# Coefficient tile allocated ahead of the weight pool: every weight tile starts 32 bytes later

## Chip, cores and metric

The kernel runs on one core of one Trainium2 chip. The metric is device time in microseconds of one execution. Before the change three runs took 1612.5, 1613.8 and 1614.32 us; their median, 1613.8 us, is the time to compare with.

## What is computed

Three stages run one after the other on 6016 tokens (2 sequences of 3008), all in float32:

```
scores = (1/S) * z @ z.T            # z: 3008 x 64 per sequence
x  = u * (max(scores, 0)**2 @ v)    # u, v: 3008 x 256 per sequence
h  = x @ w_in1                      # 256 -> 2048
x  = where(h > 0, h, exp(min(h, 0)) - 1) @ w_out1     # 2048 -> 256
h  = x @ w_in2
g  = (a0 + a1*h + a2*h^2 + a3*h^3) / (1 + |b0|*|h| + |b1|*h^2 + 1e-6)
out = g @ w_out2
```

The weights come as float64. The six coefficients a0 to a3, b0, b1 are scalars.

## The kernel before

Each float32 product is made of three matmuls on pairs of tiles: every operand is held as a rounded part (hi) and a remainder (lo), and hi*hi, hi*lo and lo*hi are added in PSUM. So TensorE (PE) issues 9240 matmuls, each with a weight load of its own (PEld).

The stationary operand of a matmul is `lhsT`, the moving one is `rhs`. In this kernel they come from these places:

- Scores (`scores`, L292): both operands are slices of the split z tiles, which lie in pool `sp` (names rl, x, t, r). The contraction is 64 long, so two matmuls stand side by side, one on the lower and one on the upper 64 rows. A pair is one step of the array.
- Attention times v (`values`, L329): stationary is the split v, which lies in pool `wp` (name w); moving is the squared score (hl and x, in `sp`). Again pairs of 64 rows.
- The two feed-forward layers (`hidden`, L399 to L402, and `project` with `mm3`, L263 to L265): stationary is a split weight in `wp` (w); moving is the activation in `sp` (rl, hl, x). The contraction is 128 long, and there are no pairs.
- In the last token tile alone the second layer's result also goes into tiles of `wp` (`second` with form "last"), so that there both operands of L263 to L265 are named w (`psum<-w`).

The moving operand is 512 columns wide in most of the work. In the attention each sequence is cut into five blocks of 512 and one of 448. In the feed-forward layers the tokens are cut into nine tiles of 512 columns and then one each of 448, 384, 320 and 256. A tile passes 16 groups (fewer of double width in the narrow ones), and the second layer of a tile runs beside the first layer of the next.

Pools are laid out in SBUF in the order in which they are entered, and the tiles of a pool behind each other. `wp` holds 32 tiles of 4096 bytes in each partition, `cp` one tile of 24 bytes that takes up 32 (`coef`), `sp` all the rest, in tiles of 2048 or 4096 bytes. The order of the instructions is written out by the code itself (`tc.manual_schedule()`); no planner depends on addresses.

Of the kernel before, what the change touches and what calls it, by code (L numbers as in the profile page):

```python
# [21 lines left out]
def attention_then_two_ffns(  # L22
# [56 lines left out]
    NG = [NF // g for g in PER]  # L79
    NSL = -(-S // W)  # L80

    wp = ctx.enter_context(tc.tile_pool(name="wp", bufs=32))
    cp = ctx.enter_context(tc.tile_pool(name="cp", bufs=1))
    sp = ctx.enter_context(tc.tile_pool(name="sp", bufs=2))
    dp = ctx.enter_context(tc.tile_pool(name="dp", bufs=1, space=bass.MemoryType.DRAM))
    ps = ctx.enter_context(tc.tile_pool(name="ps", bufs=1, space=bass.MemoryType.PSUM))
# [739 lines left out]
```

## Time and profile before

| | before |
|---|---|
| median of three runs | 1613.8 us |
| span of the profiled execution | 1611.0 us |
| PE busy | 1569.5 us, 97% of the span |
| DVE (VectorE) busy | 1392.3 us, 86% |
| ACT (ScalarE) busy | 1326.0 us, 82% |
| POOL (GpSimd) busy | 723.9 us, 45% |

The page gives the profiled execution's span, from the first to the last instruction; the 2.8 us up to the median of the runs lie around it. The attention takes the time up to about 521 us, the feed-forward layers the rest; the tiles narrower than 512 columns begin at about 1269 us with the first layer of the 448-wide one. Matmuls overlap: the duration of one is longer than the distance to the next. What a matmul costs a busy PE is the distance from start to start, which the view of instructions in order of time gives. There each row is a run of equal instructions with its start, the time to the last end, and the count.

### The profile page before, as it was taken

The numbers are of one execution on the slowest core, as the hardware profiler recorded it, in microseconds if no ns is written. First come the engines' busy times: TensorE is split into PE (matmuls) and PEld (weight loads), VectorE is DVE, ScalarE is ACT, GpSimd is POOL, SyncE is SP. The second block draws the span as 40 slices with busy tenths as digits, with TensorE's granted clock in tenths as the row PEclk, the third lists the DMA queues.
The fourth block names the chain that finished last, engine by engine and source line by source line (L and its number), as shares of the span: only waits on it lengthen the run. The fifth ranks groups of instructions, "written<-read, shape, count | busy, mean of one in ns | idle before, by whom it ended". The sixth has DMA issues, their size and how long they took to land.

```text
span 1611.0 us, 25201 instructions
## 1 busy us (share of the span) xinstructions
PE 1569.5 (97%) x9240; PEld 1321.5 (82%) x9240; DVE 1392.3 (86%) x1915; ACT 1326.0 (82%) x2123; POOL 723.9 (45%) x590
## 2 busy tenths in 40 slices
PE   8999999999999999999999999999999999999986
PEld 6888897898778778787878787887878888999976
DVE  7788889888886478989898988889898999999998
ACT  6777776877776788988888888988888888999886
POOL 3344542443433444445444444444454444444445
PEclk9999999999999999999999999999999999999999
DMA  4243343221222400000000000000000000000000
GB/s 125 66 125 119 112 144 109 66 68 50 75 61 89 157 26 1 27 1 1 27 1 27 1 27 1 27 0 1 25 1 23 1 22 1 20 1 12 11 1 15
DMA packets 38716, 67.16 MB, mean 42 GB/s; under 512 B 4928, under 2 KB 15680, under 8 KB 38592
## 3 DMA queue, kind: packets, MB, share of 16 engines
q1 hardware_dynamic: 38592, 65.55, 13.1%
q8 instruction: 72, 1.18, 0.3%
q14 instruction: 52, 0.43, 0.1%
HBM read 45.88 MB, written 19.66 MB: 41 GB/s over the span
## 4 chain that ended last, share of the span: by engine, by line
PE 66%; DVE 11%; issue 3%; ACT 3%; POOL 1%; POOLq 0%; ACTq 0%; DVEq 0%
PE psum L329 11%; PE psum L264 9%; PE psum L399 9%; PE psum L402 9%; PE psum L265 9%; PE psum L400 9%; PE psum L263 9%; PE psum L292 3%; DVE x L526 2%; DVE t L528 1%; DVE q L503 1%; DVE q L527 1%; DVE e L432 1%; DVE t L509 1%; ACT t L480 1%
## 5 line engine op out<-in xcount | busy, mean ns | idle before, releaser
L533 POOL TENSOR_TENSOR x<-t,r 128x512 fp32r<-128x512 f32 (+3 forms) x190 | 233.9, 1231 | 509.4 <-DVE t L528 443.3
L329 PE MATMUL psum<-hl,w 64*128 64x512 f32 (+1 forms) x2256 | 395.2, 391 | 3.7 <-ACT xo L349 2.6
L329 PEld LDWEIGHTS psum<-hl,w 64*128 64x128 f32 x2256 | 279.7, 185 | 44.4 <-ACT xo L349 6.4
L329 PE MATMUL psum<-x,w 64*128 64x512 f32 (+1 forms) x1128 | 293.1, 388 | 1.0 <-DVE x L305 1.0
L441 POOL TENSOR_TENSOR hl<-e,hl 128x512 fp32r<-128x512 f32 (+3 forms) x200 | 246.8, 1234 | 35.4 <-ACT hl L440 29.6
L295 ACT ACTIVATE w<-psum 128x1024 f32<-128x1024 f32 (+1 forms) x144 | 145.5, 1011 | 111.3 <-PE psum L292 109.8
L298 DVE SCALAR_TENSOR_TENSOR psum<-psum,w 128x1024 f32<-128x1024 f32 (+1 forms) x144 | 173.8, 1207 | 57.9 <-ACT w L295 57.2
L480 ACT ACTIVATE t<-psum,coef 128x512 f32<-128x512 f32 (+3 forms) x200 | 150.6, 753 | 78.8 <-PE psum L402 77.4
L503 DVE SCALAR_TENSOR_TENSOR q<-q,coef,psum 128x512 f32<-128x512 f32 (+3 forms) x190 | 135.3, 712 | 72.1 <-ACT q L496 71.5
L305 DVE TENSOR_TENSOR x<-psum,hl 128x1024 fp32r<-128x1024 f32 (+1 forms) x144 | 172.9, 1201 | 12.0 <-ACT q L200 0.5
L329 PEld LDWEIGHTS psum<-x,w 64*128 64x128 f32 x1128 | 168.0, 185 | 17.3 <-DVE x L305 1.5
L264 PE MATMUL psum<-hl,w 128*128 128x512 f32 (+4 forms) x416 | 157.2, 378 | 4.8 <-POOL hl L441 4.5
L399 PE MATMUL psum<-x,w 128*128 128x512 f32 (+4 forms) x416 | 155.6, 376 | 2.0 <-ACT x L451 1.4
L264 PE MATMUL psum<-x,w 128*128 128x512 f32 (+3 forms) x384 | 147.8, 385 | 8.5 <-POOL x L533 8.5
L263 PE MATMUL psum<-hl,w 128*128 128x512 f32 (+4 forms) x416 | 155.6, 374 | 0.2 <-ACT hl L440 0.2
L399 PE MATMUL psum<-rl,w 128*128 128x512 f32 (+4 forms) x416 | 155.5, 376 | 0.0
L265 PE MATMUL psum<-hl,w 128*128 128x512 f32 (+4 forms) x416 | 155.3, 373 | 0.0
L400 PE MATMUL psum<-x,w 128*128 128x512 f32 (+4 forms) x416 | 154.7, 374 | 0.0
L400 PE MATMUL psum<-rl,w 128*128 128x512 f32 (+4 forms) x416 | 154.4, 373 | 0.0
L296 ACT ACTIVATE hl<-w 128x1024 fp32r<-128x1024 f32 (+1 forms) x144 | 150.6, 1046 | 4.6
L432 DVE SCALAR_TENSOR_TENSOR e<-e,psum 128x512 f32<-128x512 f32 (+3 forms) x200 | 129.8, 649 | 27.8 <-ACT e L427 21.8
L526 DVE SCALAR_TENSOR_TENSOR x<-t,coef,r 128x512 fp32r<-128x512 f32 (+3 forms) x190 | 150.2, 791 | 0.0
(143 smaller groups left out, 3683.2 us busy)
## 6 DMA issues: line engine op xcount, KB each, us to landing
raw<-w_in_dram SPq DMA_DIRECT2D x16, 512.0 KB, 3.9
raw<-w_out_dram SPq DMA_DIRECT2D x16, 512.0 KB, 3.8
wd<-q SPq DMA_DIRECT2D x28, 256.0 KB, 2.3
raw<-wd SPq DMA_DIRECT2D x14, 512.0 KB, 3.4
raw<-v_dram SPq DMA_DIRECT2D x22, 256.0 KB, 2.9
raw<-uT_dram SPq DMA_DIRECT2D x10, 512.0 KB, 3.8
xd<-xo SPq DMA_DIRECT2D x20, 256.0 KB, 2.2
outT_dram<-xo SPq DMA_DIRECT2D x18, 256.0 KB, 2.2
```

The source lines that it names most:

```text
L263: nc.tensor.matmul(out, lhsT=lh, rhs=rh, start=start, stop=False)
L264: nc.tensor.matmul(out, lhsT=lh, rhs=rl, start=False, stop=False)
L265: nc.tensor.matmul(out, lhsT=ll, rhs=rh, start=False, stop=stop)
L298: nc.vector.scalar_tensor_tensor(out=s, in0=s, scalar=SCALE, in1=e, op0=ALU.mult, op1=ALU.mult)
L305: nc.vector.tensor_tensor(out=lo[:, :, :w], in0=psum[:, i:i + 2, :w], in1=f(hi[:, :, :w]), op=ALU.subtract)
L329: nc.tensor.matmul(acc[ti][d, h][:, :w], lhsT=lhs[rows, j % 2, d * P:(d + 1) * P], rhs=rhs[rows, :w], start=j == 0 and k == 0, stop=k == 2 ...
L399: nc.tensor.matmul(h[:, cols], lhsT=wh[:, d, c], rhs=x[d][0], start=d == 0, stop=False)
L400: nc.tensor.matmul(h[:, cols], lhsT=wl[:, d, c], rhs=x[d][0], start=False, stop=False)
L441: nc.gpsimd.tensor_tensor(out=lo, in0=e, in1=f(hi), op=ALU.subtract)
L480: act(new("p", "t", 3), h, AF.Identity, bias=a2, scale=a3)
L526: stt(out=st["hi"], in0=st["top"], scalar=a0, in1=st["r"], op0=ALU.add, op1=ALU.mult)
L533: eng.tensor_tensor(out=st["lo"], in0=st["p"], in1=st["r"], op=ALU.mult)
```

## The change

Two lines change places: pool `cp` is entered before pool `wp` instead of behind it.

```diff
+    cp = ctx.enter_context(tc.tile_pool(name="cp", bufs=1))
     wp = ctx.enter_context(tc.tile_pool(name="wp", bufs=32))
-    cp = ctx.enter_context(tc.tile_pool(name="cp", bufs=1))
     sp = ctx.enter_context(tc.tile_pool(name="sp", bufs=2))
```

The instructions of all five engines are the same, row for row and in the same order. Only addresses in SBUF differ. In the built programs they are (bytes in a partition):

```
            before                          after
coef        147584          (128 mod 512)   16512           (128 mod 512)
wp          16512 + 4096*i  (128 mod 512)   16544 + 4096*i  (160 mod 512)
sp          147616 ...      (160 mod 512)   147616 ...      (160 mod 512)
```

Slices of these tiles that a matmul reads start at multiples of 512 bytes in the tile. So before, a stationary operand in `wp` lies at 128 modulo 512 and a moving one in `sp` at 160; after, both lie at 160. The scores had both at 160 already, and still have. The last tile's `psum<-w` matmuls had both at 128 and have both at 160.

## Rows read from the trace of the kernel before

**Rows 1.** The page: busy time and share of each engine; chain by engine.

```profile
PE 1569.5 (97%) x9240; PEld 1321.5 (82%) x9240; DVE 1392.3 (86%) x1915; ACT 1326.0 (82%) x2123; POOL 723.9 (45%) x590
PE 66%; DVE 11%; issue 3%; ACT 3%; POOL 1%; POOLq 0%; ACTq 0%; DVEq 0%
```

**Rows 2.** Windows: start:end, length, busy us (count) by engine, clock, DMA, GB/s.

```profile
100.00:522.00 422.00, 414.54 (x3527) 359.30 (x3524) 359.30 (x373) 314.94 (x381) 177.75 (x141) 1.00 0.30 92
740.00:830.00 90.00, 89.95 (x386) 72.06 (x385) 80.07 (x118) 78.28 (x132) 42.65 (x33) 1.00 0.04 12
1280.00:1370.00 90.00, 89.85 (x412) 76.83 (x411) 83.24 (x126) 80.75 (x144) 42.17 (x35) 1.00 0.03 11
1370.00:1450.00 80.00, 79.01 (x416) 74.01 (x415) 75.83 (x126) 73.40 (x143) 37.56 (x35) 1.00 0.03 11
1520.00:1577.00 57.00, 47.98 (x335) 44.62 (x333) 54.68 (x101) 47.95 (x101) 22.17 (x23) 1.00 0.03 8
1578.50:1581.50 3.00, 3.00 (x15) 2.83 (x14) 2.90 (x5) 2.32 (x6) 2.93 (x3) 0.50 0.00 0
1582.00:1590.00 8.00, 7.93 (x67) 7.73 (x67) 7.26 (x11) 6.61 (x12) 5.19 (x4) 1.00 0.11 40
```

**Rows 3.** PE in order of time, attention, 512 columns: start, us, what, count.

```profile
15.46 0.86 PE L292 MATMUL psum<-rl 64*128 64x512 f32 x6
16.14 0.64 PE L329 MATMUL psum<-hl,w 64*128 64x512 f32 x4
16.61 0.40 PE L329 MATMUL psum<-x,w 64*128 64x512 f32 x2
...
18.94 0.86 PE L292 MATMUL psum<-rl,x 64*128 64x512 f32 x6
19.62 0.64 PE L329 MATMUL psum<-hl,w 64*128 64x512 f32 x4
```

**Rows 4.** PE in order of time, feed-forward layers, 512 columns.

```profile
900.01 0.40 PE L263 MATMUL psum<-x,w 128*128 128x512 f32 x1
...
902.35 0.63 PE L402 MATMUL psum<-x,w 128*128 128x512 f32 x2
902.81 0.40 PE L263 MATMUL psum<-hl,w 128*128 128x512 f32 x1
```

**Rows 5.** PE in order of time, attention, 448 columns.

```profile
222.98 0.81 PE L292 MATMUL psum<-r,rl 64*128 64x448 f32 x6
223.59 1.14 PE L329 MATMUL psum<-hl,w 64*128 64x448 f32 x4
...
485.55 0.78 PE L329 MATMUL psum<-hl,w 64*128 64x448 f32 x4
...
488.03 0.98 PE L292 MATMUL psum<-r,x 64*128 64x448 f32 x6
```

**Rows 6.** PE in order of time, last tile, 256 columns.

```profile
1579.26 0.42 PE L400 MATMUL psum<-x,w 128*128 128x256 f32 x1
...
1581.18 0.57 PE L402 MATMUL psum<-x,w 128*128 128x256 f32 x2
...
1584.44 0.28 PE L399 MATMUL psum<-x,w 128*128 128x256 f32 x1
...
1585.86 0.28 PE L263 MATMUL psum<-w 128*128 128x256 f32 x1
...
1592.76 0.28 PE L265 MATMUL psum<-w 128*128 128x256 f32 x1
...
1593.96 0.28 PE L263 MATMUL psum<-w 128*128 128x256 f32 x1
```

**Rows 7.** Groups by line and shape: count, busy us, mean ns, idle before.

```profile
L329 PE MATMUL psum<-hl,w 64*128 64x512 f32 x1880 | 337.3, 395 | 2.8 <-ACT xo L349 1.7 <-ACT hl L296 0.9
L329 PE MATMUL psum<-x,w 64*128 64x512 f32 x940 | 253.6, 392 | 1.0 <-DVE x L305 1.0
L329 PE MATMUL psum<-hl,w 64*128 64x448 f32 x376 | 57.9, 370 | 0.9 <-ACT xo L349 0.8
L329 PE MATMUL psum<-x,w 64*128 64x448 f32 x188 | 39.6, 365 | 0.0
L399 PE MATMUL psum<-rl,w 128*128 128x512 f32 x288 | 114.9, 399 | 0.0
L399 PE MATMUL psum<-rl,w 128*128 128x448 f32 x32 | 11.8, 369 | 0.0
```

## The prediction

> **What bounds the kernel now.** I read the page's busy line first, then windows stage by stage, then PE in order of time. TensorE is busy 97% of the span, and the chain that ended last runs through PE for 66% of it [rows 1]. In the middle of the feed-forward layers nothing else counts: in the window 740 to 830 us PE is busy 89.95 of 90 us at granted clock 1.00, with 386 matmuls, which is 90/386 = 0.2332 us for each [rows 2]. DVE is next with 80.07 of 90 us. In the attention PE is busy 414.54 of 422 us [rows 2]. Only in the last narrow tiles (47.98 of 57 us) does PE stand idle while DVE is nearly full (54.68 of 57) [rows 2]. So what matters is the distance from one matmul's start to the next, and the number of matmuls.
>
> The reader should look for the distance in the order of time, since the 0.40 us that a row gives for one matmul overlaps the next. Twelve matmuls of the feed-forward layers, from 900.01 to 902.81 us, take 2.80 us: 233.3 ns each [rows 4]. At the clock's upper level, 2.4 GHz, 512 columns are 213.3 ns, so 20 ns come on top. They are not a fixed part of a matmul: at the lower level (granted clock 0.50 in the window 1578.5 to 1581.5) nine 256-column matmuls between 1579.26 and 1581.18 us take 1.92 us, 213.3 ns each, which is 256 columns at 1.2 GHz and nothing more [rows 2, 6].
>
> **The change part by part.** No instruction, wait or DMA is added, removed or moved. coef keeps its offset modulo 512, `sp` keeps its addresses; all that can change is the speed of instructions that touch `wp`. The trace of before holds the case after already: the scores read both operands at 160 modulo 512, while the products with v read stationary ones at 128 and moving ones at 160. These two stand next to each other, same width, same 64-row pairs:
>
> - L292, both at 160: 15.46 to 16.14 us for 3 pairs, 226.7 ns a pair; again 18.94 to 19.62 us, 226.7 ns [rows 3].
> - L329, 128 against 160: 16.14 to 18.94 us for 24 matmuls or 12 pairs, 233.3 ns a pair [rows 3].
>
> The difference is 6.67 ns, 16 columns at 2.4 GHz. The 128-row matmuls of the feed-forward layers have the same 233.3 ns as the pairs with unequal offsets [rows 3, 4], so I take rows as without influence, and give them the same 6.67 ns. At 448 columns: both at 160, 222.98 to 223.59 us, 3 pairs, 203.3 ns; unequal, 485.55 to 488.03 us, 12 pairs, 206.7 ns [rows 5]: 3.3 ns. At 256 columns the sign turns: unequal, 1584.44 to 1585.86 us, 12 matmuls, 118.3 ns; both at 128, 1592.76 to 1593.96 us, 10 matmuls, 120.0 ns [rows 6]: 1.7 ns dearer. One reading fits most of it: with equal offsets a matmul costs its columns plus about 32, whatever the width (512: 544 columns are 226.7 ns; 256: 288 are 120.0 ns); with unequal ones the addition grows with the width, from 28 (118.3 ns) to 48 (233.3 ns).
>
> The sum, against the profiled execution's span of 1611.0 us:
>
> 1. Attention. L329 has 1880 + 940 = 2820 matmuls of 512 columns, 1410 pairs, and 376 + 188 = 564 of 448, 282 pairs [rows 7]. 1410 x 6.67 ns = 9.4 us, 282 x 3.3 ns = 0.9 us. PE is idle for 1.8% here and waits now and then on ACT and DVE, which do not get faster, so I let nine tenths through: 9.3 us. Bounds: 0 (others take it back) and 10.3.
> 2. Feed-forward, 512 columns. Twelve groups like L399's, each 288 [rows 7]: 3456 x 6.67 ns = 23.0 us. The cover to ask about is DVE: of a 90 us window it fills 80.07; in the 87.4 us which that window becomes (386 x 6.67 ns = 2.6 us less) it fills 91.6%. In the window 1280 to 1370 it fills 83.24 of 90, 92.5%, and PE still loses only 0.15 us [rows 2]. So all of it passes. Bounds: 23.0 more and 23.0 less, the latter if 128-row matmuls follow the 256-column row (third rival).
> 3. 448 columns. 12 x 32 = 384 matmuls [rows 7] x 3.3 ns = 1.3 us. Here DVE already fills 75.83 of 80 us and PE idles 1.0 [rows 2]: half, 0.6 us. Bounds 0 and 1.3.
> 4. 384, 320 and 256 columns, and the end. No row shows equal offsets at 384 and 320. The 256-column row gives +1.7 ns, the 448-column row -3.3 ns; for 384 matmuls of each of two widths that is +1.3 to -2.6 us, and for the 256-column ones (of 384, the 96 with both operands in w are equal already) 288 x 1.7 ns = +0.5 us. DVE sets the pace there, so I take 0.
> 5. Other engines. ACT, DVE and POOL read and write `wp` in the attention (the ReLU tile, the splits of v and the weights). They wait less than PE there: DVE 359.30 and ACT 314.94 of 422 us [rows 2]. Their instructions' durations could move either way by some ns; PE hides them. 0, bounds +-1 us.
>
> 9.3 + 23.0 + 0.6 = 32.9 us. Span 1611.0 - 32.9 = 1578.1 us; with the 2.8 us between span and median, 1580.9, say **1581 us**.
>
> **The rivals.**
>
> *No change: the offsets are not the cause.* Scores and products with v differ in more than the offset: the stationary operand of L292 lies high in SBUF with the moving one, that of L329 lies low, at 16512 to 147584. If the region decides, moving by 32 bytes does nothing and the time is 1613.8 us. Against it: 1.92 us for nine matmuls at the lower clock shows a loss that comes from two streams at speed, and region as such gives no reason why 256-column matmuls with both operands low should be the slower ones. The Trainium skill speaks for this rival: its page "SBUF — State Buffer", section "Who interferes with whom", gives TensorE two SBUF read ports, one for the moving operand and one for the weight load, that are independent, and says that PE never waits on anyone; by that rule an offset between the two could not matter. Its page "TensorE: Matmul & The Clock Gate", section "Back-to-back issue gap", gives columns/2.4 + 2.5 ns, 215.8 ns for 512. The trace does not agree: 226.7 and 233.3 ns at the same width and clock, with different operands.
>
> *Only the pairs gain.* All rows at 512 columns with equal offsets are 64-row pairs. If full-height matmuls gain nothing, term 1 alone stays: 1613.8 - 9.3 = 1604.5 us. Against it, 233.3 ns in both forms at unequal offsets.
>
> *Slower: equal offsets hurt full-height matmuls.* The only full-height rows with equal offsets are the 256-column ones, 120.0 against 118.3 ns. If their addition (32 on 256, one in eight) is a rate, 512 columns cost 576 columns, 240.0 ns: 3456 x 6.67 = 23.0 us lost in term 2, 9.3 gained in term 1, 1613.8 + 13.7 = 1627.5 us. It decides from 236.0 ns a matmul on, where 3456 x 2.7 ns eats the 9.3 us. Against it: 226.7 ns for L292 contradicts such a rate, unless pairs are apart.
>
> *The gain is taken back by DVE.* If PE, once faster, waits for DVE at its 91.6%, about half of term 2 goes: 9.3 + 11.5 + 0.3 = 21.1 us, 1592.7 us. Against it the window 1280 to 1370.
>
> **How the numbers follow.** Forecast 0.75, for itself 1574 (every term whole, with 2.6 us at 384 and 320 and 1 us from the others: 10.3 + 23.0 + 1.3 + 2.6 + 1 = 38.2, so 1575.6, and a little for the spread of the runs) to 1588 (terms 1 and 2 four fifths: 25.9). DVE rival 0.05, pairs only 0.07, no change 0.06, slower 0.07. The range from 1573 to 1600 us leaves out the last three, 0.20. Faster by over 0.2% (3.2 us, about what a measurement tells from no change): 0.75 + 0.05 + 0.07 = 0.87; within it 0.06; slower 0.07.
>
> **What would show it.** In order of time, L329 pairs at 226.7 ns like L292's and twelve feed-forward matmuls in 2.72 instead of 2.80 us; a 90 us window there with about 397 matmuls instead of 386 and DVE near 82.5 us; 256-column matmuls near 120 ns. The forecast is wrong if the 512-column feed-forward matmuls stay at 233 ns (first two rivals) or exceed it (third), or if they are at 226.7 ns but PE shows new waits on DVE or ACT (fourth).

## The result and the profile after

The changed kernel takes 1585.7 us, the median of 4 runs (1584.0 to 1586.6); before took 1613.15 us in the 4 runs beside it. The ratio is 0.9829 with an interval of 0.9815 to 0.9843, a gain of 27.5 us. The forecast was 32.9 us less, 1581 us. The mechanism came as described, and two terms of the sum were too large.

The page of the changed kernel, busy time by engine and the chain by engine, against [rows 1]:

```profile
PE 1539.6 (97%) x9240; PEld 1311.2 (83%) x9240; DVE 1390.2 (88%) x1915; ACT 1325.3 (84%) x2123; POOL 722.8 (46%) x590
PE 66%; DVE 10%; ACT 4%; issue 3%; POOL 2%; POOLq 0%; ACTq 0%; DVEq 0%
```

PE's busy time falls by 29.9 us with the same 9240 matmuls; DVE, ACT and POOL keep theirs to within 2.1 us. The profiled span is 1584.8 us, 26.2 less than before's.

PE of the changed kernel in order of time (start, us, what, count): the attention at 512 columns, against [rows 3].

```profile
19.83 0.84 PE L292 MATMUL psum<-rl,x 64*128 64x512 f32 x6
20.51 0.62 PE L329 MATMUL psum<-hl,w 64*128 64x512 f32 x4
20.96 0.39 PE L329 MATMUL psum<-x,w 64*128 64x512 f32 x2
...
23.23 0.84 PE L292 MATMUL psum<-rl,x 64*128 64x512 f32 x6
```

The three pairs of L292 (six matmuls, two by two) still take 0.68 us (19.83 to 20.51), 226.7 ns each. The twelve pairs of L329 now take 2.72 us (20.51 to 23.23) in place of 2.80: they too are at 226.7 ns. The feed-forward layers, against [rows 4]:

```profile
720.22 0.39 PE L263 MATMUL psum<-x,w 128*128 128x512 f32 x1
...
722.94 0.39 PE L263 MATMUL psum<-hl,w 128*128 128x512 f32 x1
723.69 0.50 PE L264 MATMUL psum<-hl,w 128*128 128x512 f32 x1 [0.36 <-POOL hl L441]
724.03 0.39 PE L265 MATMUL psum<-hl,w 128*128 128x512 f32 x1
```

Twelve matmuls take 2.72 us, 226.7 ns each: full-height matmuls gain what the pairs gain. But the step from L263 at 722.94 to L264 takes 0.75 us, where POOL's L441 is named as the releaser; that is one of the places where the gain is lost (below). The narrower ones, 448 columns in the attention and 256 in the last tile, against [rows 5, 6]:

```profile
483.82 0.62 PE L329 MATMUL psum<-hl,w 64*128 64x448 f32 x4
...
486.05 0.46 PE L329 MATMUL psum<-x,w 64*128 64x448 f32 x2
...
1557.87 0.28 PE L399 MATMUL psum<-x,w 128*128 128x256 f32 x1
...
1558.59 0.28 PE L263 MATMUL psum<-w 128*128 128x256 f32 x1
...
1560.03 0.28 PE L263 MATMUL psum<-w 128*128 128x256 f32 x1
```

Eleven pairs of 448 columns take 2.23 us, 202.7 ns in place of 206.7. At 256 columns both kinds, `x,w` (6 matmuls in 0.72 us) and `w` alone (12 in 1.44 us), are at 120.0 ns: the `x,w` ones, at 118.3 before, did become dearer, as forecast.

Windows of the changed kernel (start:end, length, busy us and count of PE, PEld, DVE, ACT, POOL, granted clock, DMA, GB/s), against [rows 2]:

```profile
740.00:830.00 90.00, 89.63 (x396) 73.92 (x395) 82.21 (x122) 80.40 (x137) 43.04 (x34) 1.00 0.04 12
98.20:101.40 3.20, 3.20 (x18) 2.52 (x16) 2.84 (x3) 1.35 (x2) 3.12 (x3) 0.50 0.22 82
```

396 matmuls stand in the 90 us (about 397 were forecast, 386 before) with DVE at 82.21 us (forecast 82.5). PE's busy time is 0.3 us shorter than before's in the same window: new idle time. The second row is a stretch of the attention at granted clock 0.50, dealt with below.

### The profile page after: what moved, and what is told of

The parts are those of the page before. It is cut to its first block, busy times and chain, and to the rows that moved or that the text cites. A ratio compares the mean times of both kernels' runs of the same rounds, so it can differ in the third digit from the quotient of the medians.

```text
span 1584.8 us, 25201 instructions
## 1 busy us (share of the span) xinstructions
PE 1539.6 (97%) x9240; PEld 1311.2 (83%) x9240; DVE 1390.2 (88%) x1915; ACT 1325.3 (84%) x2123; POOL 722.8 (46%) x590
## 4 chain that ended last, share of the span: by engine, by line
PE 66%; DVE 10%; ACT 4%; issue 3%; POOL 2%; POOLq 0%; ACTq 0%; DVEq 0%
PE psum L329 11%; PE psum L264 9%; PE psum L399 9%; PE psum L402 9%; PE psum L400 9%; PE psum L265 9%; PE psum L263 8%; PE psum L292 3%; DVE x L526 1%; DVE t L528 1%; DVE q L503 1%; DVE q L527 1%; POOL hl L441 1%; DVE t L509 1%; DVE e L432 1%
## 5 line engine op out<-in xcount | busy, mean ns | idle before, releaser
L533 POOL TENSOR_TENSOR x<-t,r 128x512 fp32r<-128x512 f32 (+3 forms) x190 | 233.3, 1228 | 491.3 <-DVE t L528 359.7
L329 PE MATMUL psum<-hl,w 64*128 64x512 f32 (+1 forms) x2256 | 383.5, 388 | 4.2 <-ACT xo L349 3.1
L329 PEld LDWEIGHTS psum<-hl,w 64*128 64x128 f32 x2256 | 265.7, 186 | 46.0 <-ACT xo L349 7.4
L329 PE MATMUL psum<-x,w 64*128 64x512 f32 (+1 forms) x1128 | 276.8, 385 | 0.5 <-DVE x L305 0.5
L441 POOL TENSOR_TENSOR hl<-e,hl 128x512 fp32r<-128x512 f32 (+3 forms) x200 | 247.2, 1236 | 34.8 <-ACT hl L440 33.4
L305 DVE TENSOR_TENSOR x<-psum,hl 128x1024 fp32r<-128x1024 f32 (+1 forms) x144 | 172.9, 1201 | 12.0 <-ACT q L200 0.5
L329 PEld LDWEIGHTS psum<-x,w 64*128 64x128 f32 x1128 | 156.5, 186 | 16.9 <-DVE x L305 1.3
L264 PE MATMUL psum<-hl,w 128*128 128x512 f32 (+4 forms) x416 | 155.5, 374 | 8.0 <-POOL hl L441 7.9
L399 PE MATMUL psum<-x,w 128*128 128x512 f32 (+4 forms) x416 | 153.1, 370 | 2.1 <-ACT x L451 1.4
L263 PE MATMUL psum<-hl,w 128*128 128x512 f32 (+4 forms) x416 | 153.7, 369 | 0.3 <-ACT hl L440 0.3
L265 PE MATMUL psum<-hl,w 128*128 128x512 f32 (+4 forms) x416 | 153.4, 369 | 0.0
L264 PE MATMUL psum<-x,w 128*128 128x512 f32 (+3 forms) x384 | 145.9, 380 | 7.3 <-POOL x L533 7.3
L399 PE MATMUL psum<-rl,w 128*128 128x512 f32 (+4 forms) x416 | 152.9, 370 | 0.0
L400 PE MATMUL psum<-x,w 128*128 128x512 f32 (+4 forms) x416 | 152.9, 370 | 0.0
L400 PE MATMUL psum<-rl,w 128*128 128x512 f32 (+4 forms) x416 | 152.5, 369 | 0.0
L526 DVE SCALAR_TENSOR_TENSOR x<-t,coef,r 128x512 fp32r<-128x512 f32 (+3 forms) x190 | 150.4, 792 | 0.0
```

The source lines that it names most:

```text
L263: nc.tensor.matmul(out, lhsT=lh, rhs=rh, start=start, stop=False)
L264: nc.tensor.matmul(out, lhsT=lh, rhs=rl, start=False, stop=False)
L265: nc.tensor.matmul(out, lhsT=ll, rhs=rh, start=False, stop=stop)
L305: nc.vector.tensor_tensor(out=lo[:, :, :w], in0=psum[:, i:i + 2, :w], in1=f(hi[:, :, :w]), op=ALU.subtract)
L329: nc.tensor.matmul(acc[ti][d, h][:, :w], lhsT=lhs[rows, j % 2, d * P:(d + 1) * P], rhs=rhs[rows, :w], start=j == 0 and k == 0, stop=k == 2 ...
L399: nc.tensor.matmul(h[:, cols], lhsT=wh[:, d, c], rhs=x[d][0], start=d == 0, stop=False)
```

## The experiments

Two questions: what about the operands' places decides, and where 5 us of the forecast went. The first seven kernels ran once each, the first four beside one run of before and the other three beside nine; the last five ran four or five times each, and two of them are the changed kernel unaltered. Runs of before lie between 1611.6 and 1615.7 us, so a single run settles differences of ten us and more, and none of one or two.

**Both operands at 0.** The change brings two things: equal offsets, and `wp` at 160 in place of 128. A larger `coef` puts both pools at 0 modulo 512.

```diff
-    coef = cp.tile([P, 6], F32, name="coef")
+    coef = cp.tile([P, 96], F32, name="coef")
```

> coef is given 384 bytes instead of 32, so that wp and sp both start at 0 modulo 512: equal offsets as after the change (both 160), at another place. Theory R (the offset of the stationary operand against the moving one decides): everything as after the change, 226.7 ns for a 512-column matmul or pair, about 1586 us. Theory A (the stationary operand's own start decides, 160 cheap, 128 dear, as a multiple of 64 it would be dear): 233.3 ns in all stages, L292 too, about 1616 us.

**Unequal again, the moving operand 32 bytes lower.** A pool behind `wp` moves `sp` alone. Before, the stationary operand lay 32 bytes lower than the moving one; here it lies 32 higher (160 against 128).

```diff
-    sp = ctx.enter_context(tc.tile_pool(name="sp", bufs=2))
+    gp = ctx.enter_context(tc.tile_pool(name="gp", bufs=1)); sp = ctx.enter_context(tc.tile_pool(name="sp", bufs=2))
...
-    coef = cp.tile([P, 6], F32, name="coef")
+    coef = cp.tile([P, 6], F32, name="coef"); gp.tile([P, 120], F32, name="gap")
```

> An unused tile of 480 bytes lies between wp and sp: stationary operands in wp stay at 160 modulo 512, moving ones in sp go to 128. The difference is 32 bytes as before the change, with the other sign; L292 still has both at 128. Theory R: L329 and the feed-forward layers dearer than 226.7 ns at 512 columns, near 233 ns if the sign does not matter, about 1613 us; L292 226.7 ns. Theory A: L329 and feed-forward stay at 226.7 ns, about 1586 us, and L292, now with both at 128, goes to 233 ns.

**Half the supposed period.** The same with a gap of 256 bytes (64 floats): 160 against 416.

> An unused tile of 256 bytes between wp and sp: stationary 160, moving 416 modulo 512, a difference of 256 bytes. Theory R with 512 bytes as the period: dearer than 226.7 ns, about 1600 to 1615 us. Theory M (a shorter period: 64, 128 or 256 bytes): equal again, 226.7 ns, about 1586 us. Theory A: 226.7 ns too.

**64 bytes apart.** The same with a gap of 448 bytes (112 floats): 160 against 96.

> An unused tile of 448 bytes between wp and sp: stationary 160, moving 96 modulo 512, a difference of 64 bytes. Theory R with a period over 64 bytes: not 226.7 ns at 512 columns; if the extra grows with the distance it is more than 233.3 ns and the time over 1613 us, if any unequal offset is alike 233.3 ns and about 1613 us. Theory M with a period of 64 bytes, and theory A: 226.7 ns, about 1586 us.

The window 740 to 830 us of the four kernels, in this order:

```profile
740.00:830.00 90.00, 89.64 (x396) 73.91 (x395) 82.23 (x121) 80.46 (x137) 44.20 (x35) 1.00 0.04 13
```

```profile
740.00:830.00 90.00, 89.95 (x386) 72.14 (x385) 80.06 (x118) 78.29 (x133) 42.59 (x33) 1.00 0.04 12
```

```profile
740.00:830.00 90.00, 89.64 (x396) 73.91 (x395) 82.24 (x122) 80.53 (x137) 44.47 (x35) 1.00 0.04 12
```

```profile
740.00:830.00 90.00, 89.94 (x386) 72.17 (x385) 80.06 (x118) 78.32 (x133) 42.70 (x34) 1.00 0.04 12
```

396, 386, 396, 386 matmuls; the times are 1583.8, 1613.0, 1585.2 and 1612.8 us. Equal offsets at another place are as fast as the changed kernel, so it is not the place by itself. 32 bytes to the other side are as slow as before, and 64 bytes too. And 256 bytes apart is as fast as equal: what counts is the difference modulo 256 (or a divisor of it above 64), not modulo 512 as the prediction has it. The region is out as well: in all four `wp` lies low and `sp` high.

**A fan of differences.** Tiles of `wp` are 32 bytes longer, so that each starts 32 bytes further modulo 512 and one kernel holds all multiples of 32. Differences are from here on the stationary operand's address less the moving one's, modulo 512.

```diff
-        return wp.tile([P, 2, W], dt, tag="w", name="w")
+        return wp.tile([P, 2 * W + 8], dt, tag="w", name="w")[:, 0:0 + 2 * W].rearrange("p (t w) -> p t w", t=2)
```

> Every tile of wp takes 4128 instead of 4096 bytes, so that the 32 weight tiles start at sixteen different places modulo 512, 32 bytes apart, while the moving operands stay at 160: one run shows all differences that are multiples of 32 bytes. Theory R with a period of 256 bytes: six matmuls of 512 columns in a row on one weight tile cost 226.7 ns each on the tiles at differences 0 and 256 and 233.3 ns on the fourteen others; the time comes near 1609 us. With a period of 128 bytes four of sixteen are cheap, near 1606 us. If the cost grows with the distance, values between or above appear.

1607.6 us, with 387 matmuls in the window. PE in order of time in two stretches of this kernel, weights first at a difference of 256 and then at 384:

```profile
702.29 0.40 PE L399 MATMUL psum<-x,w 128*128 128x512 f32 x1
...
704.79 0.39 PE L265 MATMUL psum<-hl,w 128*128 128x512 f32 x1
...
736.08 0.39 PE L399 MATMUL psum<-x,w 128*128 128x512 f32 x1
...
738.41 0.63 PE L402 MATMUL psum<-x,w 128*128 128x512 f32 x2
```

11 matmuls in 2.50 us, 227.3 ns, and 10 in 2.33 us, 233.0 ns. All 512-column matmuls of the feed-forward layers, grouped by the addresses of the built program (mean distance to the next matmul, without waits and without stretches at the lower clock, by the difference of the next stationary operand from the moving one): 0 gives 229.4 ns, 256 gives 228.4, 192 and 448 give 230.6 and 230.5, and all the other multiples of 32, 128 and 384 among them, 232.3 to 233.7. So the period is 256, not 128. The means at 0 and 256 lie over 226.7 mainly at the ends of a tile's six matmuls: inside such a tile the first distance is 231.6 ns on average, the next four are 227.1 to 228.3, and the one to the next tile is 230.9. A matmul's neighbours thus act on its distance.

**The fan, moved by 16 bytes.** The same tiles read from their fifth float (`[:, 4:4 + 2 * W]`).

> As the run with 4128-byte tiles, and the data start 16 bytes into each tile: differences of 16, 48, 80 ... bytes. If equality within one line of some bytes is enough, differences of 16 and 272 are as cheap as 0 (226.7 ns); if the start itself must agree, no weight tile is cheap, all are at 233.3 ns or more, and the time is 1613 us or more.

1606.2 us, 389 matmuls in the window. Neither expected outcome came: by the same grouping, differences of 240 and 496 give 227.9 and 228.1 ns, 176, 400 and 432 give 229.1 to 230.5, and 16 and 272 give 231.7 and 233.0. In this mixture sixteen bytes short of equality is still cheap, sixteen beyond is not. But 144, which is 256 bytes from 400, gives 232.9 where 400 gives 229.1: this run alone does not bear out the period for every difference. Since neighbours act on each other here, it does not settle how the distance changes within 32 bytes either.

**A difference of 192 alone.** The gap pool with 320 bytes (80 floats): 160 against 480, so that the stationary operand is 64 bytes below the moving one modulo 256.

> An unused tile of 320 bytes between wp and sp: stationary 160, moving 480 modulo 512, a difference of 192 bytes for all matmuls with a weight in wp. In the run with sixteen places the tiles at 192 and 448 stood at 230.6 and 230.5 ns, between cheap and dear, but beside other differences. If that is a value of its own, all 512-column matmuls cost some 230 ns here and the time is about 1600 us; if it was a trace of the neighbours, they cost 226.7 or 233.3 ns and the time is 1586 or 1613 us.

```profile
740.00:830.00 90.00, 89.73 (x393) 73.31 (x392) 81.52 (x120) 79.89 (x136) 43.05 (x34) 1.00 0.04 12
```

1594.4 us with 393 matmuls, 90/393 = 229.0 ns: a value of its own between 226.7 and 233.2. So there are not two levels, fitting and unfitting. At 448 columns the order is another one. PE of this kernel in the attention:

```profile
480.43 0.76 PE L329 MATMUL psum<-hl,w 64*128 64x448 f32 x4
...
482.83 0.98 PE L292 MATMUL psum<-r,x 64*128 64x448 f32 x6
```

Twelve pairs take 2.40 us, 200 ns each, which is less than the 202.7 ns with equal offsets. The seven such stretches of this trace without a wait stand at 200.5 to 200.8 ns, and those of the kernel with the stationary operand 64 bytes above at 201.9 to 202.4. So of the differences tried alone, 0 and 256 are the cheapest at 512 columns, but not at 448.

**The changed kernel once more**, beside a version in which POOL's split L441 stands ahead of its L533 at the turn from one token tile to the next. The reason for the second is the 0.75 us from L263 to L264 above. The same turn before the change, PE and then POOL:

```profile
734.21 0.40 PE L263 MATMUL psum<-hl,w 128*128 128x512 f32 x1
734.65 0.50 PE L264 MATMUL psum<-hl,w 128*128 128x512 f32 x1
```

```profile
728.19 1.62 POOL L380 TENSOR_TENSOR rl<-raw,rl 128x512 fp32r<-128x512 f32 x1 [1.50 <-PE psum L265]
732.04 1.30 POOL L533 TENSOR_TENSOR x<-t,r 128x512 fp32r<-128x512 f32 x1 [2.23 <-DVE t L528]
733.30 1.29 POOL L441 TENSOR_TENSOR hl<-e,hl 128x512 fp32r<-128x512 f32 x1
```

and after it, POOL and DVE:

```profile
717.24 1.62 POOL L380 TENSOR_TENSOR rl<-raw,rl 128x512 fp32r<-128x512 f32 x1 [1.34 <-PE psum L265]
721.09 1.30 POOL L533 TENSOR_TENSOR x<-t,r 128x512 fp32r<-128x512 f32 x1 [2.23 <-ACT r L520]
722.35 1.29 POOL L441 TENSOR_TENSOR hl<-e,hl 128x512 fp32r<-128x512 f32 x1
```

```profile
717.02 0.69 DVE L380 TENSOR_TENSOR rl<-raw,rl 128x512 fp32r<-128x512 f32 x1
717.62 1.78 DVE L526 SCALAR_TENSOR_TENSOR x<-t,coef,r 128x512 fp32r<-128x512 f32 x1
719.44 0.69 DVE L527 SCALAR_TENSOR_TENSOR q<-q,x 128x512 f32<-128x512 f32 x1
720.17 0.75 DVE L528 SCALAR_TENSOR_TENSOR t<-t,coef,q 128x512 f32<-128x512 f32 x1
```

From POOL's L380, which splits the next tile, to PE's L264, which needs L441's result, it is 6.46 us before (728.19 to 734.65) and 6.45 after (717.24 to 723.69): this chain is not any faster. PE's own way from the same moment to L263 is 6.02 us before and 5.70 after. So PE now waits 0.3 us longer. In the chain stands DVE's L526 with 1.78 us, beside POOL's L380; L533 starts when DVE's L528 is through (720.17 + 0.75 us). The view names ACT's L520, but the reciprocal that L520 makes for this step is read by L526 too, and so was there before 717.62 us.

```diff
+        edge = i1 and not early and i and i[1] == NG[i[0]] - 1
         if j2:
-            second_steps(j2, "quotient", "rest")
+            second_steps(j2, "quotient")
+        if edge:
+            first_split(i1)
+        if j2:
+            second_steps(j2, "rest")
...
-        if i1 and not early:
+        if i1 and not early and not edge:
             first_split(i1)
```

> The changed kernel once more, as a control for the next one: ratio to before 0.983; spans of 1582 to 1585 us, lower by some 1.5 us for each early stretch of low granted clock that a run does not have.

> The changed kernel, and in the one step per token tile that splits the next tile's input (L380 on POOL and DVE) the remainder of the ELU output (L441 on POOL) is issued ahead of the second layer's remainder (L533) instead of behind it. Theory W (part of the gain is given back at each tile's edge, where PE's L264 waits for L441, which stands behind L533 on POOL): the wait of 0.53 us at each of eight or nine edges goes, 4 us less than the changed kernel, about 1581 us. Rival: L533 comes late in its place and PE waits for it one step later; no change.

The changed kernel took 1586.8 us (0.9827, interval 0.9814 to 0.9841), the reordered one 1590.7 (0.986, 0.9846 to 0.9874): slower by 3.9 us. DVE and PE of the reordered one:

```profile
720.15 1.78 DVE L526 SCALAR_TENSOR_TENSOR x<-t,coef,r 128x512 fp32r<-128x512 f32 x1
721.97 1.67 DVE L527 SCALAR_TENSOR_TENSOR q<-q,x 128x512 f32<-128x512 f32 x1
723.67 0.75 DVE L528 SCALAR_TENSOR_TENSOR t<-t,coef,q 128x512 f32<-128x512 f32 x1
...
730.45 0.61 PE L402 MATMUL psum<-x,w 128*128 128x512 f32 x2
731.33 0.50 PE L399 MATMUL psum<-x,w 128*128 128x512 f32 x1 [0.27 <-DVE t L510]
```

Neither theory W (4 us less) nor its rival (no change) came. Now L527 takes 1.67 us in place of 0.69 while POOL's L441 runs beside it, and PE waits for DVE's L510 a little later (L402 to L399 0.88 us for two matmuls, where 0.45 is the pace). That points away from the order on POOL and to DVE and POOL side by side, which the next two kernels try.

**Both at once, and the collision alone.** L380 has two halves, one on DVE and one on POOL. With both on DVE, POOL has nothing beside L526.

```diff
-        for d, eng in enumerate((nc.vector, nc.gpsimd)):
+        for d, eng in enumerate((nc.vector, nc.vector)):
```

The first kernel has this and the reordering, the second this alone; the control is the changed kernel.

> The changed kernel as a control for the two that follow: ratio to before 0.983, at each token tile's edge a distance of 0.75 us from L263 to L264.

> The changed kernel with L441 ahead of L533 at the tile's edge, and with both remainders of the next tile's input (L380) on DVE instead of one on POOL. Theory W2 (at the edge POOL and DVE hold each other up: L526 takes 1.78 us beside POOL's L380 and, with L441 moved, L527 takes 1.67 beside L441, against 0.8 and 0.7 alone; and L441 stands behind L533): with no POOL subtraction at the edge both waits of PE go, 4 us less than the changed kernel. Rival: the 0.7 us more on DVE delays the next group by as much; no change or up to 2 us slower.

> The changed kernel with both L380 on DVE and the order of L441 and L533 unchanged. If the order on POOL alone makes the wait of PE at the edge (L533 waits for ACT L520 until then), the 0.75 us stay and the time with them, within 1 us of the changed kernel. If the collision of POOL's L380 with DVE makes it, the wait goes and the time is 3 to 4 us less.

Control 1586.1 us (0.9826, 0.9812 to 0.9839); with the reordering 1590.9 (0.9847, 0.9832 to 0.9862); L380 alone 1582.7 (0.9805, 0.9791 to 0.9818). The first is 4.8 us slower than its control in the medians, outside both outcomes expected of it; the second came as its collision theory said. In the version with both, L441 has slid beside DVE's two halves of L380, DVE first and then POOL:

```profile
718.31 2.38 DVE L380 TENSOR_TENSOR rl<-raw,rl 128x512 fp32r<-128x512 f32 x2
...
718.60 1.55 POOL L441 TENSOR_TENSOR hl<-e,hl 128x512 fp32r<-128x512 f32 x1 [1.42 <-issue]
```

In the version with L380 alone on DVE (DVE, POOL, PE):

```profile
715.93 1.29 DVE L380 TENSOR_TENSOR rl<-raw,rl 128x512 fp32r<-128x512 f32 x2
717.13 0.75 DVE L526 SCALAR_TENSOR_TENSOR x<-t,coef,r 128x512 fp32r<-128x512 f32 x1
...
719.56 1.29 POOL L533 TENSOR_TENSOR x<-t,r 128x512 fp32r<-128x512 f32 x1 [4.77 <-DVE t L528]
720.81 1.30 POOL L441 TENSOR_TENSOR hl<-e,hl 128x512 fp32r<-128x512 f32 x1
...
721.84 0.39 PE L263 MATMUL psum<-hl,w 128*128 128x512 f32 x1
722.17 0.50 PE L264 MATMUL psum<-hl,w 128*128 128x512 f32 x1
```

The same two halves take 1.29 us when POOL is quiet, 2.38 beside L441; L526 takes 0.75 in place of 1.78; and L263 to L264 is 0.33 us in place of 0.75. The Trainium skill, "SBUF — State Buffer", section "Who interferes with whom", says that a DVE instruction with two inputs in SBUF contends with a GpSimd instruction that reads SBUF; these rows agree, for SCALAR_TENSOR_TENSOR too. This is the fastest kernel of the study, 3.4 us below its control, though the two intervals overlap a little (up to 0.9818, from 0.9812). Those of the version with both and the control overlap as well (from 0.9832, up to 0.9839), and what makes up its 4.8 us was not taken apart.

## Why the prediction was right, and where it was not

The sum is compared with the profiled execution first, stage by stage. The attention's last product with v ends just ahead of the first L263 (a few first-layer matmuls stand between the products already); this L263 before, after, and with both operands at 0:

```profile
520.66 0.50 PE L263 MATMUL psum<-hl,w 128*128 128x512 f32 x1
```

```profile
515.43 0.50 PE L263 MATMUL psum<-hl,w 128*128 128x512 f32 x1
```

```profile
512.75 0.51 PE L263 MATMUL psum<-hl,w 128*128 128x512 f32 x1
```

**Term 1, attention, 9.3 us: right in kind, mis-sized.** The pairs fell to 226.7 ns as forecast. The stage gained 5.2 us in the profiled execution and 7.9 us in the one with both at 0. The first has a stretch of 3.4 us at granted clock 0.50 (98.1 to 101.5 us, the window above; PE was busy 17.1 of the 18.1 us ahead of it), in which it lost 1.6 us; the second has none in its attention. The rest of the difference is the start: the L292 row at 19.83 us above stands at 18.94 before [rows 3] and at 18.76 in the second. Such stretches fall in other places from execution to execution (before has one at 11.4 us), and the sum took no account of them. Apart from them, "nine tenths" was too much. From that L292 row to the end of the stage it is 501.7 us before and 494.0 with both at 0, 7.7 less. The distances near the pace gave 9.8 us, and the longer ones took 2.1 back: those of over a quarter above the pace lie 22.1 us over it before and 24.2 with both at 0 (worked out from the starts of all matmuls). A part of this the profile names as waits of PE for DVE's L305 and ACT's L349, engines that did not get faster: 8.1 us before and 8.8 with both at 0.

**Term 2, feed-forward at 512 columns, 23.0 us, "so all of it passes": mis-sized.** From the end of the attention to the last matmul of 512 columns in L399 to L402 it is 844.2 us before and 823.7 after, 20.5 less. The pace outside of waits fell from 233.3 to 226.9 ns; on the 3409 distances of 512 columns in this stretch that is 22.0 us, and 184 of 448 columns that stand in it too give 0.7. Before has a stretch at the lower clock here (588.3 us, 1.5 us lost) and after has none: together 24.2. Against it stand the turns between token tiles. Of the distances from L263 to L264 at 512 columns, outside that stretch, twelve are over 262 ns; what they are above 230 ns adds up to 5.4 us before and 8.5 after, 3.1 us lost; other waits take 0.6. That gives 20.5. The cover that failed is DVE's: I judged it by its share of a window (82.21 of 90 us now), and a share does not show that a chain over POOL and DVE sets the pace once in each tile. In the version with L380 on DVE the twelve distances are ten and come to 5.0 us, 3.5 less, and its median is 3.4 us below its control.

This is the rival "taken back by DVE" at about a quarter of its size (3.1 of 11.5 us), in another place: not by DVE's share, but by one collision at each turn.

**Term 3, 448 columns, 0.6 us, and terms 4 and 5, 0.** From there to the end of the program the gain is 26.2 - 5.2 - 20.5 = 0.5 us, and 0.7 came from the 448-column matmuls ahead of that point. That is 1.2 us where the sum has 0.6; which width has which part of the last 0.5 us was not separated.

**The rivals.** "No change" by the region falls with the four kernels with displaced pools. "Only the pairs" and "slower" fall with the twelve full-height matmuls in 2.72 us. My reading of equal offsets as columns plus about 32 holds at 512 (226.7 ns) and 256 columns (120.0), but not at 448, where 202.7 ns are 38 more. Why this much remains with equal offsets is open, and so is what unequal ones hold up: the prediction's "two streams at speed" was not shown, since no kernel here changes the one stream without the other.

What the prediction drew from the rule of the Trainium skill ("SBUF — State Buffer", section "Who interferes with whom": independent read ports, PE never waits), that an offset between the two operands could not matter, does not hold in these runs: 396 against 386 matmuls in the same 90 us, by 32 bytes of offset. Whether it is the ports or something behind them the runs do not show. The 215.8 ns that the prediction set beside the rows is given by the Trainium skill ("TensorE: Matmul & The Clock Gate", section "Back-to-back issue gap") for the gap of a single isolated matmul, so it is no measure for the stream of these rows.

The modulus of 512, by which the addresses were compared ahead of the prediction, was neither tested nor doubted there. 256 bytes apart is as good, and the runs say nothing of what lies behind that. The forecast did not suffer from it, because the change makes the two offsets equal by either modulus.

## What to carry to other kernels

Where a PE-bound kernel's matmuls take longer than their columns at the granted clock, look for two lines with the same width and different operand pools, and compare their distances start to start; a difference of 3% can be a matter of 32 bytes in an allocation. For matmuls of 512 columns lay the pools of moving and stationary operands so that they agree modulo 256 bytes, and measure each width apart: at 448 columns a difference of 192 was cheaper than none (200.6 against 202.7 ns), and at 256 columns equal offsets were the dearer ones. And when the bounding engine gets faster, follow each chain through the other engines at the seams of the loop, where instructions of two tiles stand side by side: an engine's share of a window does not show them.

## What the runs showed of the hardware

- The distance between 512-column matmuls depends on the difference between the two operands' addresses: 226.7 ns at 0 and 256; 233.2 with the stationary operand 32 bytes above or below the moving one or 64 above; 229.0 with it 64 below (192 modulo 256). For multiples of 32 bytes the fan of tiles shows a period of 256.
- The order changes with the width: pairs of 448 columns took 206.5 ns with the stationary operand 32 bytes below, 202.7 at 0, 202.1 at 64 above and 200.6 at 192; 256-column matmuls took 118.3 ns at 32 below and 120.0 at 0.
- The cost is not that of the matmul alone. L292, both of whose operands lie in `sp`, is at 227 ns where its neighbours have equal offsets, and also before; but on average at 229.0 with `wp` 32 bytes above, 230.6 at 64 above and 231.3 at 192 (means over the distances from one L292 pair to the next, waits left out). In the fan of tiles the first distance after a change to a cheap tile is 231.6 ns, the next 227.8.
- A DVE instruction with two SBUF inputs beside POOL's subtraction took 1.78 in place of 0.75 us, and cost PE 0.4 us at each turn by way of POOL (0.75 against 0.33 us).
